# Splitting the first query and key loads over three queues, and moving one relu ahead of a cast, in a fused attention and gated-FFN kernel

## The chip, the cores and the metric

The kernel runs on one core of a Trainium2 chip. The metric is the device time in microseconds (us) of one execution. Before the change the median of three runs was 435.25 us (434.73 to 435.25). A profile shows one execution; its engines are TensorE (PE, with its weight loads as PEld), VectorE (DVE), ScalarE (ACT), GpSimd (POOL) and SyncE (SP). SP, ACT and POOL each have a queue of their own for DMAs.

## The reference

```
scores = (q @ k^T) / sqrt(64)              # 8 batches, 12 heads, 448 rows, 64 columns
attn   = max(scores, 0)^2 / 448            # no softmax
x      = (attn @ v), heads side by side    # 3584 rows x 768
gate   = max(x @ w_gate, 0)                # 768 -> 1536
val    = x @ w_val
out    = (gate * val) @ w_out              # 1536 -> 768
```

All inputs and the output are float32. The kernel computes in bf16 with float32 accumulation, and applies both constant factors once, squared together, when the output leaves PSUM (L294).

## The kernel before

The eight batches are handled one after the other. A batch's attention is made of score tiles of 128 keys by two heads (2 x 448 queries, one tile of two PSUM banks, tag sc, three buffers), a relu on ACT from PSUM to SBUF (L184, tile r_sb, four buffers), a square on DVE (L188, tile attn), and products with v. Heads go in pairs hp (0 to 5), and two pairs make a group qd of four heads. The FFN of a batch is a list of units: twelve gv_unit (gate and value products for 128 of the 1536 columns, L257) and then out_unit (output products, L283). From batch 1 on these units are dealt out between the attention steps, so that TensorE has matmuls while ACT and DVE work on the scores. Batch 0 has no FFN beside it: first_batch (L378) runs alone, and eight gv_units follow it.

Every instruction is pinned: each engine runs its instructions in the order in which the program lists them. Waits between engines follow from the data and the buffers.

Keys and queries arrive with rows across partitions (tiles kn and qn, [128, head, 4, 64]: partitions 0 to 63 hold four consecutive rows each, rows 0 to 255; partitions 64 to 127 hold three each, rows 256 to 447). So each load is a pair of DMAs, lo and hi. Loads on POOL's queue (dma_in, L95) cast float32 to bf16 on the way. For batches 0 to 2 TensorE transposes two heads of k and q at a time into a PSUM bank (L177), and DVE copies 960 columns (512 for k, 448 for q, the last 64 of k's 512 being padding) to SBUF (L179, tile kq_sb). Later batches are transposed by DMA, by way of the buffers kr and qr.

The start is special. load_first(4) (L97) brings the keys of heads 0 to 3 as float32 into staged, a view of the then unused buffer kr, by SP's queue (lo, L101) and ACT's (hi, L102); DVE casts them two heads at a time into kn (L107). The queries of those heads come by POOL. Then POOL makes the identity for the transposes (L91) and issues k and q of heads 4 to 7, k and q of heads 8 to 11, v, and the weights in chunks (L333 to L344). ACT, right behind its DMA, runs one relu on a blank tile (L104), which makes it load its function table early. TensorE runs 14 pairs of matmuls on blanks (L395) before the first transposes and some more between the first rounds.

In first_batch, five rounds (n = 0 to 4) make three score tiles each, transpose the next head pair, and relu and square the tiles. After that comes a tail written out by hand (L409 to L430). It has score tiles u0 to u2 (of n = 5) and w0 to w2 (of n = 6), and six products values(qd, c) with v, each in a PSUM bank of tag acc (two buffers), turned into the FFN's input xT by a cast: four on DVE, and those of values(1, 0) and values(2, 0) on ACT:

```
relu2(*u1)
w0 = tile_of(6, 0)
cast(*values(1, 0), on_act=True)
relu2(*u2)
w1 = tile_of(6, 1)
```

relu2 is one relu on ACT and one square on DVE. With the banks' reuse, the first gate product (g_ps) needs the bank of values(2, 0).

Of the kernel before, what the change touches and what calls it, by code (L numbers as in the profile page):

```python
# [9 lines left out]
FP32 = mybir.dt.float32  # L10
BF16 = mybir.dt.bfloat16
# [5 lines left out]
def kernel(  # L17
# [15 lines left out]
    nc = tc.nc  # L33

    B, H, S, D = q.shape
# [16 lines left out]
    kqpool = ctx.enter_context(tc.tile_pool(name="kqpool", bufs=3))  # L52
# [7 lines left out]
    def pin(ins):  # L60
        return tc.keep_in_program_order(ins)
# [15 lines left out]
    kn_b = [const.tile([128, H, 4, D], BF16, name=f"kn{i}") for i in range(NB)]  # L77
    qn_b = [const.tile([128, H, 4, D], BF16, name=f"qn{i}") for i in range(NB)]
    v_b = [const.tile([128, H, 4, D], BF16, name=f"vn{i}") for i in range(NB)]
    kr = const.tile([128, 4, d_model], BF16, name="kr")  # L80
    qr = const.tile([128, 4, d_model], BF16, name="qr")
    staged = kr.rearrange("p i m -> p (i m)")[:, 0:4 * 8 * D].bitcast(FP32)
    staged = staged.rearrange("p (h i d) -> p h i d", i=4, d=D)
    for n in range(NB):
        if n == 0:
            pin(nc.vector.memset(staged[64:128, :, 3, :], 0.0))
        for t in (kn_b[n], qn_b[n]):
            pin(nc.vector.memset(t[64:128, :, 3, :], 0.0))

    def make_ident():  # L90
        pin(nc.gpsimd.affine_select(out=ident, in_=ident, compare_op=ALU.not_equal, fill=1.0, base=0,  # L91
                                    pattern=[[-1, 128]], channel_multiplier=1))

    def dma_in(o, i):
        pin(nc.gpsimd.dma_start(out=o, in_=i))  # L95

    def load_first(h1):  # L97

        lo = k[0, 0:h1, 0:256, :].rearrange("h (j i) d -> j h i d", i=4)
        hi = k[0, 0:h1, 256:448, :].rearrange("h (j i) d -> j h i d", i=3)  # L100
        pin(nc.sync.dma_start(out=staged[0:64], in_=lo))  # L101
        pin(nc.scalar.dma_start(out=staged[64:128, :, 0:3, :], in_=hi))  # L102

        pin(nc.scalar.activation(rpool.tile([128, 2, S], BF16, name="r_sb")[:, 0, :], blank, AF.Relu))  # L104
        load_nat(qn_b[0], q, 0, 0, h1)
        for h in range(0, h1, 2):
            pin(nc.vector.tensor_copy(kn_b[0][:, h:h + 2], staged[:, h:h + 2]))  # L107

    def load_nat(dst, src, b, h0, h1):
        lo = src[b, h0:h1, 0:256, :].rearrange("h (j i) d -> j h i d", i=4)  # L110
        hi = src[b, h0:h1, 256:448, :].rearrange("h (j i) d -> j h i d", i=3)
        dma_in(dst[0:64, h0:h1, :, :], lo)
        dma_in(dst[64:128, h0:h1, 0:3, :], hi)

    def load_qk(b, h0=0, h1=H):
        load_nat(kn_b[b % NB], k, b, h0, h1)
        load_nat(qn_b[b % NB], q, b, h0, h1)

    def load_v(b):
        load_nat(v_b[b % NB], v, b, 0, H)  # L120

    def low_values(b):

        t = v_b[b % NB].rearrange("p (q s h) i d -> p q s h i d", s=2, h=2)
        pin(nc.vector.tensor_copy(t[64:128, :, 1, :, 3, :], t[0:64, :, 1, :, 3, :]))
# [31 lines left out]
    def operands(b, hp, bank=None):  # L157

        if b >= PE_B:
            n = b % NB  # L160
            return kT_b[n][:, hp, 0:S], qT_b[n][:, hp, 0:S]
        kq = transposes(b, hp, bank)
        return kq[:, 0:S], kq[:, 512:512 + S]

    def sc_tile():
        return psum.tile([128, 2, 512], FP32, name="sc_ps", tag="sc", bufs=3)
# [1 line left out]
    def transposes(b, hp, bank):  # L168
        if bank is None:
            ps = psum.tile([128, 2048], BF16, name="kq_ps", tag="sc", bufs=3)  # L170
        else:
            ps = bank.bitcast(BF16)
        for t, c0 in ((kn_b[b % NB], 0), (qn_b[b % NB], 512)):
            for i in range(4):
                for h2 in range(2):
                    o = ps[h2 * 64:h2 * 64 + 64, c0 + i * 128:c0 + i * 128 + 128]
                    pin(nc.tensor.transpose(o, t[:, 2 * hp + h2, i, :], ident))  # L177
        kq = kqpool.tile([128, 512 + S], BF16, name="kq_sb")
        pin(nc.vector.tensor_copy(kq, ps[:, 0:512 + S]))  # L179
        return kq  # L180

    def relu_part(src, n):
        r = rpool.tile([128, 2, S], BF16, name="r_sb")[:, :n, :]
        pin(nc.scalar.activation(r, src, AF.Relu))  # L184
        return r

    def square_part(dst, r):
        pin(nc.vector.tensor_tensor(dst, r, r, ALU.mult))  # L188

    def relu2(src, dst, n):  # L190
        square_part(dst, relu_part(src, n))
# [31 lines left out]
    def av_pair(b, qd, c, attn, ps):  # L223

        p = HALVES[c][1]
        for h2, o in HALVES:
            mm(ps[o, :S], v_b[b % NB][p, 4 * qd + 2 * c + h2, 3, :], attn[p, 6 + h2, :], True, False)
        for i in range(3):
            for h2, o in HALVES:
                mm(ps[o, :S], v_b[b % NB][:, 4 * qd + 2 * c + h2, i, :], attn[:, 8 * c + 2 * i + h2, :], False, i == 2)  # L230

    def bank_tile():
        return psum.tile([128, 512], FP32, name="xT_ps", tag="acc", bufs=2)

    def idle_matmuls(ps, n):

        for _ in range(n):
            mm2(ps[:, :S], blank[:, 0:128], blank, True, True)
# [86 lines left out]
    def gap():  # L325
# [4 lines left out]
        flush()  # L330
        share[2] = i + 1

    load_first(4)  # L333
    make_ident()
    load_qk(0, 4, 8)
    load_qk(0, 8, H)
    load_v(0)
    load_gv(0)
    load_gv(1)
# [14 lines left out]
    def transpose_pair(b, hp, bank=None):  # L354
        kqs[b, hp] = operands(b, hp, bank)

    def attn_of(b, qd):
        if (b, qd) not in attns:
            attns[b, qd] = atpool.tile([128, 14, S], BF16, name="attn")
        return attns[b, qd]  # L360

    def burst(b, tiles):

        todo, begun = [], None
        for qd, kind, c, i in tiles:
            attn = attn_of(b, qd)
            if kind == "pair":
                todo.append(scores(kqs[b, 2 * qd + c], i, attn, 8 * c + 2 * i))
            elif kind == "last":
                todo.append(scores_last((kqs[b, 2 * qd], kqs[b, 2 * qd + 1]), attn))  # L370
            else:
                ps = sc_tile()
                banks = [ps[:, c, :S] for c in range(2)]
                av_last(b, qd, attn, banks)
                begun = (qd, banks, ps[:, :, :S])
        return todo, begun

    def first_batch():  # L378

        def tile_of(n, i):  # L380
            return burst(0, [tiles_first[3 * n + i]])[0][0]

        def values(qd, c):
            ps, x = bank_tile(), xT_of[0][:, 2 * qd + c, :]
            av_pair(0, qd, c, attn_of(0, qd), ps)
            return x, ps[:, :S]

        def cast(x, ps, on_act=False):
            if on_act:
                pin(nc.scalar.activation(x, ps, AF.Copy))  # L390
            else:
                pin(nc.vector.tensor_copy(x, ps))

        bank = bank_tile()
        idle_matmuls(bank, 14)  # L395
        transpose_pair(0, 0, bank)
        bank = bank_tile()
        idle_matmuls(bank, 4)
        for n in range(5):
            t = [tile_of(n, i) for i in range(3)]  # L400
            if n == 4:
                low_values(0)
            transpose_pair(0, n + 1, bank)
            if n < 4:
                bank = bank_tile()
                idle_matmuls(bank, 2)
                for u in t:
                    relu2(*u)
        relu2(*t[0])  # L409
        relu2(*t[1])  # L410
        u0 = tile_of(5, 0)
        cast(*values(0, 0))
        relu2(*t[2])
        u1 = tile_of(5, 1)
        cast(*values(0, 1))
        u2 = tile_of(5, 2)
        relu2(*u0)
        relu2(*u1)
        w0 = tile_of(6, 0)
        cast(*values(1, 0), on_act=True)  # L420
        relu2(*u2)
        w1 = tile_of(6, 1)
        cast(*values(1, 1))
        w2 = tile_of(6, 2)
        relu2(*w0)
        relu2(*w1)
        x, ps = values(2, 0)
        relu2(*w2)
        cast(x, ps, on_act=True)
        cast(*values(2, 1))  # L430
# [45 lines left out]
    for b in range(B):  # L476
        xT_of[b] = xpool.tile([128, KD, S], BF16, name="xT")
        if b == 0:
            first_batch()
        else:  # L480
            batch(b)
        if b + 1 < B:
            ffn.extend(ffn_units(b))
            if b == 0:
                for _ in range(7):
                    ffn.pop(0)()
                for hp in range(2):
                    midway.append(lambda hp=hp: transpose_pair(1, hp))
                ffn.pop(0)()
# [34 lines left out]
```

## Time and profile before

| | us |
|---|---|
| median of three runs | 435.25 |
| the profiled execution, in whole | 435.1 |
| its span in the profile | 433.3 |
| PE busy | 425.4 (98%) |
| PEld busy | 250.3 (58%) |
| ACT busy | 218.0 (50%) |
| DVE busy | 210.7 (49%) |
| POOL busy | 49.0 (11%) |
| first score relu starts | 7.74 |
| first gate product starts | 27.04 |

The granted TensorE clock is 0.9 or more of full speed in all forty slices of the span. The DMA engines are busy 90% or more in each of the first eight slices, which is up to about 87 us, and have gaps after that. A row of the timeline gives the start, the length (of the whole group when several are merged), engine, line, operation, output and input, and in brackets the idle time ahead of it with what ended it. A share of DMA above 1 means several packets in flight on an engine. The size of a DMA, and GB/s, count bytes as written: a load that casts float32 to bf16 reads twice as many (47.19 MB were read from memory in all). A busy PE is not a PE at its peak, since the ends of pipelined matmuls are modelled; the waits say more than the shares.

### The profile page before, as it was taken

What the parts mean: (1) busy time and instruction counts of PE and PEld (TensorE: products, weight loads), DVE (VectorE), ACT (ScalarE), POOL (GpSimd) and SP (SyncE); (2) the same over time, 40 slices, a digit from 0 to 9 for tenths busy, and PEclk for the clock granted to TensorE, in tenths of its full rate; (3) what the DMA queues carried; (4) which work ended last, traced back from release to release, by engine and by line L of the source; (5) the groups of instructions that cost most, each with busy time, mean ns of one, the idle gap of its engine ahead of it and who ended that gap; (6) DMA issues with size and microseconds to landing.
All of it is one profiled execution on the core that took longest, in us unless ns stands there. A gap on an engine that the chain in (4) does not pass through costs nothing.

```text
span 433.3 us, 11436 instructions
## 1 busy us (share of the span) xinstructions
PE 425.4 (98%) x5068; PEld 250.3 (58%) x5068; DVE 210.7 (49%) x334; ACT 218.0 (50%) x325; POOL 49.0 (11%) x71
## 2 busy tenths in 40 slices
PE   8899999999999999999999999999999999999996
PEld 4457655655565555655566555655566555566564
DVE  5952784556623655356532565435643454422210
ACT  4942666454554564465454645554545645532221
POOL 8424311100204000300004000010000000000001
PEclk9999999999999999999999999999999999999999
DMA  9999999905679770591517932170414100030014
GB/s 151 181 205 195 203 205 211 204 5 81 106 145 166 103 112 19 104 198 34 97 38 128 176 66 65 38 138 2 101 29 106 42 2 2 12 100 2 2 38 109
DMA packets 78513, 42.45 MB, mean 98 GB/s; under 512 B 48352, under 2 KB 74976, under 8 KB 78464
## 3 DMA queue, kind: packets, MB, share of 16 engines
q0 software_dynamic: 45120, 23.47, 40.6%
q1 hardware_dynamic: 32992, 18.01, 17.8%
q8 instruction: 39, 0.64, 0.6%
q10 hardware_dynamic: 352, 0.25, 0.2%
q14 instruction: 10, 0.08, 0.1%
HBM read 47.19 MB, written 11.01 MB: 134 GB/s over the span
## 4 chain that ended last, share of the span: by engine, by line
PE 84%; DMA 12%; POOL 2%; issue 1%; POOLq 0%; ACT 0%
PE o_ps L64 25%; PE g_ps L64 23%; PE v_ps L64 22%; PE sc_ps L64 13%; DMA qn<-in_q_dram 5%; DMA wo<-in_moe_w_out_dram 5%; DMA vn<-in_v_dram 2%; POOL qn L95 1%; PE kq_ps L177 1%; POOL kn L95 1%; POOL vn L95 0%; POOL out_dram L302 0%; POOLq L519 0%; ACT o_sb L294 0%; POOL ident L91 0%
## 5 line engine op out<-in xcount | busy, mean ns | idle before, releaser
L184 ACT ACTIVATE r_sb<-sc_ps 128x896 bf16<-128x896 f32 x168 | 145.1, 927 | 39.4 <-PE sc_ps L64 39.4
L188 DVE TENSOR_TENSOR attn<-r_sb 128x896 bf16<-128x896 bf16 x168 | 103.7, 623 | 92.2 <-ACT r_sb L184 92.1
L64 PE MATMUL g_ps<-xT,wg 128*64 128x448 bf16 x1152 | 126.1, 354 | 0.0
L64 PE MATMUL v_ps<-xT,wv 128*64 128x448 bf16 x1152 | 125.2, 352 | 0.0
L64 PE MATMUL o_ps<-wo,hT 128*64 128x384 bf16 (+1 forms) x1368 | 115.3, 324 | 0.3 <-DMA wo<-in_moe_w_out_dram 0.3
L271 DVE TENSOR_TENSOR hT<-v_ps,g_sb 128x448 bf16<-128x448 f32 x96 | 59.9, 624 | 88.4 <-PE v_ps L64 87.5
L64 PEld LDWEIGHTS <-hT 128*64 128x64 bf16 x1368 | 75.5, 110 | 37.8 <-issue 6.5
L265 ACT ACTIVATE g_sb<-g_ps 128x448 bf16<-128x448 f32 x96 | 52.3, 545 | 88.9 <-PE g_ps L64 88.9
L64 PEld LDWEIGHTS <-wg 128*64 128x64 bf16 x1152 | 63.4, 110 | 49.8 <-issue 13.1
L64 PEld LDWEIGHTS <-wv 128*64 128x64 bf16 x1152 | 66.2, 110 | 41.0
L294 ACT ACTIVATE o_sb<-o_ps 128x384 f32<-128x384 f32 (+1 forms) x57 | 27.9, 489 | 81.4 <-PE o_ps L64 81.4
L64 PE MATMUL sc_ps<-attn,vn 128*64 128x448 bf16 (+1 forms) x336 | 35.1, 354 | 0.0
L95 POOL DMA_DIRECT2D vn<-in_v_dram x16 | 12.1, 768 | 168.5 <-PE sc_ps L64 161.0
L458 DVE CAST xT<-sc_ps 128x896 bf16<-128x896 f32 x21 | 22.9, 1091 | 14.3 <-PE sc_ps L64 14.3
L64 PEld LDWEIGHTS <-vn 128*64 128x64 bf16 (+1 forms) x384 | 18.8, 109 | 16.5 <-issue 5.6
L64 PE MATMUL sc_ps<-qT,kT 64*64 64x448 bf16 x420 | 28.4, 357 | 0.0
L64 PE MATMUL sc_ps<-kq_sb 64*64 64x448 bf16 x252 | 19.0, 360 | 1.9 <-ACT r_sb L184 1.7
L95 POOL DMA_DIRECT2D kn<-in_k_dram x18 | 13.3, 762 | 46.8 <-PE kq_ps L177 45.2
L64 PEld LDWEIGHTS <-kT 64*64 64x64 bf16 x420 | 9.6, 105 | 14.3 <-issue 11.7
L302 POOL DMA_DIRECT2D out_dram<-o_sb x2 | 1.1, 558 | 146.2 <-ACT o_sb L294 146.2
L95 POOL DMA_DIRECT2D qn<-in_q_dram x20 | 14.6, 752 | 9.4 <-DMA vn<-in_v_dram 6.3
L64 PEld LDWEIGHTS <-kq_sb 64*64 64x64 bf16 x252 | 6.5, 105 | 13.3 <-issue 9.9
(32 smaller groups left out, 84.2 us busy)
## 6 DMA issues: line engine op xcount, KB each, us to landing
out_dram<-o_sb SPq DMA_DIRECT2D x54, 192.0 KB, 2.7
vn<-in_v_dram POOLq DMA_DIRECT2D x8, 384.0 KB, 7.7
kn<-in_k_dram POOLq DMA_DIRECT2D x7, 384.0 KB, 9.7
qn<-in_q_dram POOLq DMA_DIRECT2D x7, 384.0 KB, 12.2
vn<-in_v_dram POOLq DMA_DIRECT2D x8, 288.0 KB, 8.7
wo<-in_moe_w_out_dram POOLq DMA_DIRECT2D x2, 1152.0 KB, 20.0
kn<-in_k_dram POOLq DMA_DIRECT2D x7, 288.0 KB, 10.9
qn<-in_q_dram POOLq DMA_DIRECT2D x7, 288.0 KB, 13.0
```

The source lines that it names most:

```text
L64: pin(nc.tensor.matmul(o, lhsT=l, rhs=r, start=start, stop=stop, skip_group_check=True))
L95: pin(nc.gpsimd.dma_start(out=o, in_=i))
L177: pin(nc.tensor.transpose(o, t[:, 2 * hp + h2, i, :], ident))
L184: pin(nc.scalar.activation(r, src, AF.Relu))
L188: pin(nc.vector.tensor_tensor(dst, r, r, ALU.mult))
L265: pin(nc.scalar.activation(g_sb, g_ps, AF.Relu))
L271: pin(nc.vector.tensor_tensor(hT[:, mf, col:col + S], v_ps, g_sb, ALU.mult))
L294: pin(nc.scalar.activation(out=o_sb[:, c0:c1], in_=o_ps, func=AF.Copy, scale=float(out_scale)))
L302: pin(e.dma_start(out=segment_rows(b0, 2 * t + s)[:, m], in_=o_sb[s * 64:s * 64 + 64, m]))
L458: pin(nc.vector.tensor_copy(xT_of[b][:, 2 * qd:2 * qd + 2, :], both))
```

## The change

Four things are changed.

- load_first now has three pairs of float32 loads on SP's and ACT's queues: keys of heads 0 and 1, queries of heads 0 and 1, keys of heads 2 and 3. A second view, of the buffer qr, stages the queries, and two of its heads get a clearing memset. POOL brings only the queries of heads 2 and 3 there. DVE has three casts instead of two.
- POOL then loads the keys of heads 4 to 11 in one pair of DMAs, followed by the queries of heads 4 to 7 and of heads 8 to 11. Before, it was two pairs for keys and two for queries.
- In the tail of the first batch ACT's relu of tile u2 comes ahead of ACT's cast of values(1, 0). TensorE's and DVE's order stays.
- kq_sb holds 2 x 448 columns instead of 960, and the copy reads two pieces of 448 out of PSUM.

```diff
--- before.py
+++ after.py
@@ -79,11 +79,14 @@
     v_b = [const.tile([128, H, 4, D], BF16, name=f"vn{i}") for i in range(NB)]
     kr = const.tile([128, 4, d_model], BF16, name="kr")
     qr = const.tile([128, 4, d_model], BF16, name="qr")
-    staged = kr.rearrange("p i m -> p (i m)")[:, 0:4 * 8 * D].bitcast(FP32)
-    staged = staged.rearrange("p (h i d) -> p h i d", i=4, d=D)
+    staged = []
+    for grp in (kr, qr):
+        st = grp.rearrange("p i m -> p (i m)")[:, 0:4 * 8 * D].bitcast(FP32)
+        staged.append(st.rearrange("p (h i d) -> p h i d", i=4, d=D))
     for n in range(NB):
         if n == 0:
-            pin(nc.vector.memset(staged[64:128, :, 3, :], 0.0))
+            pin(nc.vector.memset(staged[0][64:128, :, 3, :], 0.0))
+            pin(nc.vector.memset(staged[1][64:128, 0:2, 3, :], 0.0))
         for t in (kn_b[n], qn_b[n]):
             pin(nc.vector.memset(t[64:128, :, 3, :], 0.0))
 
@@ -94,17 +97,19 @@
     def dma_in(o, i):
         pin(nc.gpsimd.dma_start(out=o, in_=i))
 
-    def load_first(h1):
-
-        lo = k[0, 0:h1, 0:256, :].rearrange("h (j i) d -> j h i d", i=4)
-        hi = k[0, 0:h1, 256:448, :].rearrange("h (j i) d -> j h i d", i=3)
-        pin(nc.sync.dma_start(out=staged[0:64], in_=lo))
-        pin(nc.scalar.dma_start(out=staged[64:128, :, 0:3, :], in_=hi))
+    def load_first():
+
+
+        for st, src, h in ((staged[0], k, 0), (staged[1], q, 0), (staged[0], k, 2)):
+            lo = src[0, h:h + 2, 0:256, :].rearrange("h (j i) d -> j h i d", i=4)
+            hi = src[0, h:h + 2, 256:448, :].rearrange("h (j i) d -> j h i d", i=3)
+            pin(nc.sync.dma_start(out=st[0:64, h:h + 2], in_=lo))
+            pin(nc.scalar.dma_start(out=st[64:128, h:h + 2, 0:3, :], in_=hi))
 
         pin(nc.scalar.activation(rpool.tile([128, 2, S], BF16, name="r_sb")[:, 0, :], blank, AF.Relu))
-        load_nat(qn_b[0], q, 0, 0, h1)
-        for h in range(0, h1, 2):
-            pin(nc.vector.tensor_copy(kn_b[0][:, h:h + 2], staged[:, h:h + 2]))
+        load_nat(qn_b[0], q, 0, 2, 4)
+        for st, t, h in ((staged[0], kn_b[0], 0), (staged[1], qn_b[0], 0), (staged[0], kn_b[0], 2)):
+            pin(nc.vector.tensor_copy(t[:, h:h + 2], st[:, h:h + 2]))
 
     def load_nat(dst, src, b, h0, h1):
         lo = src[b, h0:h1, 0:256, :].rearrange("h (j i) d -> j h i d", i=4)
@@ -160,7 +165,7 @@
             n = b % NB
             return kT_b[n][:, hp, 0:S], qT_b[n][:, hp, 0:S]
         kq = transposes(b, hp, bank)
-        return kq[:, 0:S], kq[:, 512:512 + S]
+        return kq[:, 0, :], kq[:, 1, :]
 
     def sc_tile():
         return psum.tile([128, 2, 512], FP32, name="sc_ps", tag="sc", bufs=3)
@@ -175,8 +180,8 @@
                 for h2 in range(2):
                     o = ps[h2 * 64:h2 * 64 + 64, c0 + i * 128:c0 + i * 128 + 128]
                     pin(nc.tensor.transpose(o, t[:, 2 * hp + h2, i, :], ident))
-        kq = kqpool.tile([128, 512 + S], BF16, name="kq_sb")
-        pin(nc.vector.tensor_copy(kq, ps[:, 0:512 + S]))
+        kq = kqpool.tile([128, 2, S], BF16, name="kq_sb")
+        pin(nc.vector.tensor_copy(kq, ps[:, 0:1024].rearrange("p (t c) -> p t c", t=2)[:, :, 0:S]))
         return kq
 
     def relu_part(src, n):
@@ -330,10 +335,11 @@
         flush()
         share[2] = i + 1
 
-    load_first(4)
+    load_first()
     make_ident()
-    load_qk(0, 4, 8)
-    load_qk(0, 8, H)
+    load_nat(kn_b[0], k, 0, 4, H)
+    load_nat(qn_b[0], q, 0, 4, 8)
+    load_nat(qn_b[0], q, 0, 8, H)
     load_v(0)
     load_gv(0)
     load_gv(1)
@@ -417,8 +423,9 @@
         relu2(*u0)
         relu2(*u1)
         w0 = tile_of(6, 0)
-        cast(*values(1, 0), on_act=True)
+        second = values(1, 0)
         relu2(*u2)
+        cast(*second, on_act=True)
         w1 = tile_of(6, 1)
         cast(*values(1, 1))
         w2 = tile_of(6, 2)
```

## The prediction

> **What bounds the kernel now.** I read the chain that ended last first, then who TensorE waits for, then the chain again in order of time, then the instructions of the first 30 us, and last the DMA rate by stretch.
>
> The chain's shares by engine:
> ```profile
> PE 84%; DMA 12%; POOL 2%; issue 1%; POOLq 0%; ACT 0%
> ```
> All TensorE's waits in the whole run (total, times, longest):
> ```profile
> PE sc_ps L64 <- ACT r_sb L184: 1.7, 5, 0.4
> PE xT_ps L64 <- DVE blank L74: 1.2, 1, 1.2
> PE xT_ps L64 <- DVE attn L188: 0.7, 2, 0.4
> PE o_ps L64 <- DMA wo<-in_moe_w_out_dram: 0.3, 1, 0.3
> ```
> The chain in order of time, its first 65 us:
> ```profile
> 6.70 1.23 POOL qn L95 x2
> 7.92 0.63 POOL vn L95
> 8.55 10.05 DMA vn<-in_v_dram
> 18.60 0.28 issue
> 18.88 22.11 DMA qn<-in_q_dram
> 41.00 0.86 issue
> 41.85 21.70 DMA wo<-in_moe_w_out_dram
> 63.55 0.04 issue
> 63.60 1.17 PE o_ps L64 x12
> ```
> The reader should see three stretches. Up to 27 us TensorE waits for others. From 27.04 us to the end it is never kept waiting, but for once: the second half of w_out lands at 63.55, and the first output product, ready at 63.34, starts at 63.60 (0.26 us). So the chain that ended last does not run through the first batch at all: it runs through the loads. Whatever the first batch gains, call it G, brings that product's readiness forward to 63.34 - G, but it can't start before w_out is there. If the loads come D earlier, the gain at the end is the smaller of D and G + 0.26.
>
> The first batch, rows of the timeline:
> ```profile
> 5.33 1.01 DVE L107 CAST kn<-kr 128x512 bf16<-128x512 f32 x2 [2.14 <-DMA kr<-in_k_dram]
> 6.59 0.66 DVE L179 COPY kq_sb<-xT_ps 128x960 bf16<-128x960 bf16 x1 [0.26 <-PE xT_ps L177]
> 7.74 13.88 ACT L184 ACTIVATE r_sb<-sc_ps 128x896 bf16<-128x896 f32 x17 [4.36 <-PE sc_ps L64]
> 22.36 0.54 ACT L390 ACTIVATE xT<-xT_ps 128x448 bf16<-128x448 f32 x1 [0.74 <-PE xT_ps L64]
> 26.17 0.62 DVE L188 TENSOR_TENSOR attn<-r_sb 128x896 bf16<-128x896 bf16 x1 [0.18 <-ACT r_sb L184]
> 27.04 1.33 PE L64 MATMUL g_ps<-xT,wg 128*64 128x448 bf16 x12
> ```
> ACT is the bound of this stage: it runs 17 relus without a gap from 7.74 to 21.62, then stands 0.74 us for the value product that its cast needs.
>
> The loads, one stretch a row (length; busy us of PE, PEld, DVE, ACT, POOL; clock; DMA share; GB/s written):
> ```profile
> 8.00:9.00 1.00, 1.00 (x25) 0.64 (x21) 0.32 (x1) 1.00 (x2) 1.00 (x2) 1.00 1.45 176
> 12.00:14.00 2.00, 1.63 (x28) 0.83 (x28) 1.83 (x4) 2.00 (x3) 2.00 (x3) 1.00 1.26 148
> 20.00:25.00 5.00, 4.46 (x50) 1.69 (x46) 4.54 (x9) 4.26 (x6) 0.83 (x1) 1.00 1.24 207
> 30.00:40.00 10.00, 10.00 (x110) 7.40 (x107) 2.73 (x5) 2.42 (x5) 3.21 (x5) 1.00 1.48 196
> ```
> From about 2.5 us on the DMA engines have work all the time; only the rate differs, 362 GB/s at best while the first keys come as float32, 176 for the queries and keys after them, 139 on average from 10.5 to 14.5, then about 200.
>
> **The change part by part.** The profiled execution took 435.1 us, its span 433.3 and 1.8 around it; the median of the three runs is 435.25, their spread 0.52. The sum is made against 435.1.
>
> *Relu ahead of ACT's cast.* ACT is free at 21.62 and the scores of u2 were made at 20.87 to 21.25, so relu u2 fills the gap (pitch of relus 0.80 us) and the cast follows at about 22.42, beside the product ready at 22.31. Three relus after it by 0.80 end at 25.4 instead of 26.14. Late next would be DVE: its square of u2 moves from 23.74 to 23.22, right behind the square of u1 (ends 23.28); the cast of values (1,1) and the squares of w0 and w1 follow at a pitch of 0.54, so the square of w2 starts at 25.42 instead of 26.17. TensorE's wait for relu u2 at 23.76 (0.26 us) goes too. What is queued behind the moved relu is the cast that frees a bank, needed only by values (2,0), now at 23.9. Gain at the first gate product: 0.74 us.
>
> *First loads.* Before, k of heads 0 to 3 landed at 5.24 on SP's queue (issue 0.74, 4.5 to landing) and at 4.0 on ACT's; POOL's q of heads 0 to 3 at 6.05. Now three pairs go out on each of the two queues. One more issue costs its queue about 0.75 us (0.77 and 0.74 in the timeline). SP issues nothing else until 69 us. On ACT two more issues push the table load and the blank relu from 1.51 to about 3.0, done near 4.9; ACT's next work is at 7.74, so 2.8 us of cover hide 1.5 us. The extra clearing of two heads on DVE is half of a 0.27 us row, hidden before the first cast at 5.33. The queries' cast is new on DVE, one at about 0.5 us (two cost 1.01). TensorE can't start the transposes before the 28 idle matmuls let it, at 5.45 (0.19 behind the last, as between all of them), against 5.81: at most 0.36 to win. But DVE's queue now holds three casts ahead of the first copy, and the third, keys of heads 2 and 3, waits for the last pair. The HW queues carried 0.459 MB, the last bytes at about 4.3, landing 5.24; 0.229 MB more at 200 to 362 GB/s take 0.63 to 1.15 us, less some 0.4 since the first pair is half as long and SP's bytes, which began only at 3.0 behind ACT's, come sooner. So it lands between 5.5 and 6.0, its cast ends between 6.05 and 6.55, against a copy that started at 6.59 and at best starts at 6.23. Gain 0 to 0.36; a landing past 6.1 makes it a loss, to -0.2. I take 0.1, nearer to the contended rate, as POOL's queue begins to move at 3.7.
>
> *896-column copies.* 0.66 us for 960 columns scales to 0.62 for 896: 0.03 on the first copy, and nothing on the 17 others, hidden behind ACT (three relus take 2.43 us a round, DVE's copy and squares 2.26) or behind matmuls. The copy's two pieces of 448 could be slower than one piece. Against that stands L151, 3072 bf16 elements in runs of 64 in 0.95 us. From above: at the pace of the 448-column float32 casts (0.62 each) a copy would take about 1.1. I take 0.62.
>
> So G is 0.74 + 0.1 + 0.03, about 0.85 (0.5 to 1.15).
>
> *POOL's issues.* A four-head pair has a pitch of 1.20 us (3.00, 4.20, 5.40, 6.60, 7.80), the twelve-head pair of v 1.48. By a line through these an eight-head pair is 1.34 and a two-head pair 1.13. Two four-head pairs become one of eight (-1.06) and the first shrinks (-0.07): v and all the weights are issued 1.1 us earlier. Later issues each wait until the eighth load before them has landed (the 19th load, q of batch 1, starts at 17.16 behind v's first half, the 11th), and two loads fewer shift both alike.
>
> *What D is.* This is the disputed cost. As an issue matter D is up to 1.1. But POOL handed out 0.229 MB each 1.20 us, 191 GB/s, while 177 were moved, and time to landing grew from 3.7 to 4.4 us over those issues: the engines are slightly behind POOL, so most of the 1.1 isn't theirs to give. As a matter of bytes: queries of two heads leave POOL's queue (0.115 MB written at 177 GB/s, 0.65 us) and come as float32 (0.229 MB at 362 GB/s, 0.63 us): nothing. Counted as bytes written at the later 196 to 207 GB/s, the extra 0.115 MB costs 0.57 us. A gain lies in the pace: 177 GB/s at a share of 1.43 in 4 to 10 us against 196 at 1.48 when much was queued ahead (30 to 40 us). If larger and earlier issues bring the remaining 1.03 MB of keys and queries to 195, that is 5.83 - 5.29 = 0.54 us. Ends: -0.57 and +1.1. I take +0.3, about half of the pace's gain: the latency shows backlog, so near the middle. Sum: 435.1 - min(0.3, 1.1) = 434.8.
>
> The Trainium skill, page "DMA: Bandwidth & Descriptors", section "Issuing engines are not separate DMA queues", says that loads of all issuing engines run on the same 16 engines and interleave, and that spreading them saves only issue time. The rows agree in that 362 GB/s read is about twice the 177 written after a halving cast; by that page alone D is 0 and the time is the second rival's.
>
> **The rivals.**
> 1. The loads were paced by POOL: D reaches the cap G + 0.26 = 1.1, time 434.0 (433.7 with G 1.15). For it: the pace of 177 is near 191, and the slow stretch of 10.5 to 14.5 us ends when POOL stops issuing at 14.24, which now comes 1.1 us sooner. Against: the growing latency.
> 2. The transfer is hidden anyway: D = 0, the product waits 0.26 + G instead of 0.26, time 435.1. For it: equal bytes read, engines with work from 2.5 us on. Against: pace below that of 30 to 40 us.
> 3. Slower: w_out lands later, since the float32 queries add written bytes ahead of everything. D = -0.57, time 435.7; any D below 0 decides, because TensorE has no slack at 63.6. To come out past 0.2% it needs -0.9, so a further stall of the kind seen at 10.5 to 14.5 (139 against 196 GB/s is 1.2 us of 4): 436.3 with half of it added. Against: the float32 rows move at twice the written rate.
> 4. The cut copy falls to 1.1 us: five rounds of 2.7 instead of 2.43 and 0.45 on the first, 1.8 us lost, G = -0.95, time 435.8.
>
> **How the numbers follow.** A measurement of this kernel can tell about 0.2%, 0.87 us, from no change; faster then means below 434.4. Forecast (434.4 to 435.0) 0.38; rival 1 0.32; rival 2 0.14; rival 3 0.12; rival 4 0.04. Faster: rival 1 and a little of the forecast's edge, 0.34. Slower by over 0.2%: the part of rival 3 with a further stall and of rival 4, 0.10. Same: the rest, 0.56. The range from 433.8 to 435.9 leaves out the best case of rival 1 and the worst of rival 3. The likeliest one's own is 434.4 to 435.0.
>
> **What would show it.** Right: ACT's 0.74 gap at the cast gone, 18 relus in one run; the first gate product near 26.2; POOL's first weight issue near 8.2; and TensorE's wait for w_out at 63 us grown from 0.26 to about 0.8. Wrong: w_out landing before 62.6 (rival 1), after 63.7 (rival 3), rows of L179 above 0.7 us (rival 4), or the first copy later than 6.6 behind the third cast. Wrong as a whole if TensorE has no wait for w_out left, or new waits after 64 us.

## The result and the profile after

The changed kernel took 435.87 us (median of 20 runs, 435.14 to 436.99), the kernel before 434.91 (median of 20, 434.59 to 435.38). The ratio is 1.0019, with an interval of 1.0012 to 1.0026: the change makes the kernel slower by 0.96 us. The forecast was 0.3 us faster. The profiled execution of the changed kernel took 436.1 us, its span 434.3.

TensorE's waits after, the whole run (total, times, longest):

```profile
PE sc_ps L64 <- ACT r_sb L189: 1.6, 4, 0.4
PE xT_ps L64 <- DVE blank L74: 1.2, 1, 1.2
PE xT_ps L182 <- DVE qn L112: 1.0, 1, 1.0
PE sc_ps L64 <- DVE kq_sb L184: 0.3, 1, 0.3
PE xT_ps L64 <- DVE attn L193: 0.2, 1, 0.2
```

The wait for w_out is gone. In its place TensorE waits for DVE's cast of the queries (L112), and for the first copy (L184). The chain that ended last, in order of time, now begins at SP's queue:

```profile
1.57 0.82 SPq L106
2.39 0.04 issue
2.43 5.82 DMA kr<-in_k_dram
8.26 0.03 issue
8.28 0.02 DVEq L112
8.30 0.04 issue
8.35 0.43 DVE kn L112
8.78 0.54 DVE kq_sb L184
9.32 0.04 issue
9.36 0.76 PE sc_ps L64 x12
```

The reader should see the third pair of float32 loads, keys of heads 2 and 3, issued at 2.43 and landing only at 8.26. Its cast stands on DVE ahead of the first copy, which was done at 7.25 before and is done at 9.31 now, for heads 0 and 1, which don't need those keys. But that cast is the smaller part of the delay. The queries of heads 0 and 1, which the first copy does need, landed at 7.27, and TensorE's transposes of them ended at 8.27, against 6.55 before. Of the 2.10 us by which the first copy starts later (8.69 against 6.59), the late queries make 1.7 and the third cast 0.4. The timeline's rows of the first batch:

```profile
4.29 0.43 DVE L112 CAST kn<-kr 128x512 bf16<-128x512 f32 x1 [0.96 <-DMA kr<-in_k_dram]
7.36 0.45 DVE L112 CAST qn<-qr 128x512 bf16<-128x512 f32 x1 [2.64 <-DMA qr<-in_q_dram]
8.35 0.43 DVE L112 CAST kn<-kr 128x512 bf16<-128x512 f32 x1 [0.54 <-DMA kr<-in_k_dram]
8.69 0.62 DVE L184 COPY kq_sb<-xT_ps 128x896 bf16<-128x896 bf16 x1
9.65 0.83 POOL L98 DMA_DIRECT2D wg<-in_moe_w_gate_dram  x1 [1.20 <-DMA kn<-in_k_dram]
9.80 14.69 ACT L189 ACTIVATE r_sb<-sc_ps 128x896 bf16<-128x896 f32 x18 [5.09 <-PE sc_ps L64]
24.41 0.54 ACT L396 ACTIVATE xT<-xT_ps 128x448 bf16<-128x448 f32 x1
28.28 1.33 PE L64 MATMUL g_ps<-xT,wg 128*64 128x448 bf16 x12
```

ACT's gap ahead of its cast is gone, and 18 relus run without a break. But the first relu starts at 9.80 instead of 7.74, and the first gate product at 28.28 instead of 27.04. Two differences make up the first gate product's delay of 1.24 us: 2.06 lost before the first relu, and 0.82 won between it and the gate product (18.48 us after, 19.30 before). The two spans differ by 1.0 and not by 1.24, since the 0.26 us that TensorE waited for w_out in the profile of before are gone.

Sizes and microseconds to landing of the early loads after, for issues at 1.57 to 2.4 us:

```profile
qr<-in_q_dram SPq DMA_DIRECT2D x1, 128.0 KB, 5.7
qr<-in_q_dram ACTq DMA_DIRECT2D x1, 96.0 KB, 3.4
kr<-in_k_dram ACTq DMA_DIRECT2D x1, 96.0 KB, 5.7
qn<-in_q_dram POOLq DMA_DIRECT2D x1, 64.0 KB, 3.1
qn<-in_q_dram POOLq DMA_DIRECT2D x1, 48.0 KB, 5.4
```

and for SP's third, issued at 2.43:

```profile
kr<-in_k_dram SPq DMA_DIRECT2D x1, 128.0 KB, 5.8
```

Before, SP's single load of 256 KB had landed after 4.5 us:

```profile
kr<-in_k_dram SPq DMA_DIRECT2D x1, 256.0 KB, 4.5
```

Now half of that size takes 5.7 or 5.8, from issue to landing.

### The profile page after: what moved, and what is told of

Same layout as the page of the kernel before. It is cut to its first block, busy times and chain, and to the rows that moved or that the text cites. A ratio compares the mean times of both kernels' runs of the same rounds, so it can differ in the third digit from the quotient of the medians.

```text
span 434.3 us, 11444 instructions
## 1 busy us (share of the span) xinstructions
PE 426.2 (98%) x5068; PEld 250.2 (58%) x5068; DVE 210.3 (48%) x336; ACT 218.0 (50%) x325; POOL 48.0 (11%) x69
## 4 chain that ended last, share of the span: by engine, by line
PE 93%; DVE 3%; DMA 1%; issue 1%; ACT 1%; SPq 0%; POOL 0%; POOLq 0%; DVEq 0%
PE g_ps L64 26%; PE o_ps L64 25%; PE v_ps L64 25%; PE sc_ps L64 15%; DVE attn L193 2%; DMA kr<-in_k_dram 1%; PE kq_ps L182 1%; ACT r_sb L189 1%; DVE kq_sb L184 1%; DVE xT L398 0%; SPq L106 0%; PE xT_ps L182 0%; DVE hT L276 0%; POOL out_dram L307 0%; POOLq L526 0%
## 5 line engine op out<-in xcount | busy, mean ns | idle before, releaser
L98 POOL DMA_DIRECT2D kn<-in_k_dram x16 | 12.0, 764 | 48.7 <-PE kq_ps L182 47.5
L98 POOL DMA_DIRECT2D qn<-in_q_dram x20 | 14.5, 748 | 4.8 <-DMA vn<-in_v_dram 2.3
```

## The experiments

The theory after the result: the float32 loads land late because POOL's loads share the DMA engines with them; the relu's move is worth what was forecast; w_out is no cap. The first rival: the second and third load of a queue are slow by themselves. The second: the wait for w_out limits the kernel, and the parts act through it. "First relu" and "first gate" below are starts in the profiled execution of each kernel.

### The parts taken alone or together, loads as before

The edit of the first, against the kernel before:

```diff
-        return kq[:, 0:S], kq[:, 512:512 + S]
+        return kq[:, 0, :], kq[:, 1, :]
...
-        kq = kqpool.tile([128, 512 + S], BF16, name="kq_sb")
-        pin(nc.vector.tensor_copy(kq, ps[:, 0:512 + S]))
+        kq = kqpool.tile([128, 2, S], BF16, name="kq_sb")
+        pin(nc.vector.tensor_copy(kq, ps[:, 0:1024].rearrange("p (t c) -> p t c", t=2)[:, :, 0:S]))
...
-        cast(*values(1, 0), on_act=True)
+        second = values(1, 0)
         relu2(*u2)
+        cast(*second, on_act=True)
```

> The moved relu and the 896-column copies alone, with all loads as before. Theory (the start is late in the changed kernel because of the float32 loads; w_out is early there because of POOL's loads): first score relu at 7.7, first gate product near 26.25 (0.77 sooner), w_out lands near 63.5 as before, TensorE's wait for it grows from 0.26 to about 1.0, time within 0.2 us of before. Rival (the loads run ahead because the first batch does): w_out lands before 63.0 and the time falls by 0.5 us or more.

434.11 us against 434.89 before, ratio 0.9985 (0.9976 to 0.9994). First relu to first gate took 18.49 us. In this execution the first relu was itself late, at 8.53, which the last section comes back to, so the gate product started at 27.02 and not at 26.25. w_out landed at 63.3. That execution took 434.83 us, 0.72 above the kernel's median, so its rows are not those of a typical one. By the medians of 11 and 21 runs the time fell by 0.78 us: a forecast of no gain, on the grounds that w_out holds everything back, was wrong a second time.

Next, the relu's three lines of this edit alone, and the copies' lines alone, each against the kernel before:

> The moved relu alone. Theory (all of the 0.78 us that relu and copies gave together is the relu's): ACT's gap of 0.74 before its cast gone, first relu to first gate product 18.5 us instead of 19.3, time 0.7 to 0.8 below before. Rival (the shorter copies share in it): 0.4 us or less.

> The 896-column copies alone. Theory: 0.62 us a copy instead of 0.66, first relu to first gate product 19.3 us as before, time within 0.2 us of before. Rival (they share in the gain): 0.3 us or more below before.

The relu alone took 434.23 against 434.77, ratio 0.9985 (0.9976 to 0.9994), 18.49 us from first relu to first gate. The copies alone took 434.79, ratio 0.9999 (0.9990 to 1.0008), 19.30 us. By the medians the relu gave 0.54 us, less than the 0.7 to 0.8 expected and more than its rival's 0.4; the interval, about 0.3 to 1.0 us, holds the 0.78 as well. The copies alone show no gain, though the noise would hide one of 0.4. So the gain is the relu's as far as these runs can tell, and the timeline gives its size. It is 0.81 and not 0.74 on the timeline because a gap counts from an end to a start, while neighbours on ACT overlap: after, the cast starts at 24.41 and the relu ahead of it ends at 24.49.

### The new loads alone

The changed kernel with both parts above undone.

> The new loads alone, without the moved relu and with the 960-column copies. Theory: first score relu near 9.8 as in the changed kernel, first gate product near 29.05 (28.28 plus 0.77), no wait for w_out, time 0.8 us above the changed kernel, that is about 1.7 above before. Rival (the relu's move is worth less, since something else ends the first batch): less than 0.4 us above the changed kernel.

436.77 us against 434.89, ratio 1.0039 (1.0027 to 1.0052). First relu 9.68, first gate 28.98, 19.30 us between them. TensorE's waits:

```profile
PE xT_ps L182 <- DVE qn L112: 2.2, 1, 2.2
PE sc_ps L64 <- ACT r_sb L189: 1.7, 5, 0.4
```

So the loads cost 1.88 us by themselves, and the relu and the copies give 0.78 back; that makes 1.1 for the whole, against 0.96 measured. The time lies 0.90 above the changed kernel, near the 0.8 of the theory. This profile is also a repeat of the changed kernel's start: the queries of heads 0 and 1 landed at 7.2 and the keys of heads 2 and 3 at 7.9. With the first loads as before, the first relu starts between 7.74 and 8.53 in six profiles, so the loss before it is 1.2 to 2.1 us.

### What makes the float32 loads late

First POOL's loads were held back. The changed kernel, with the identity made first and one small copy on POOL that needs the last float32 load:

```diff
+        hold = const.tile([128, 2, 64], FP32, name="hold")
+        pin(nc.gpsimd.tensor_copy(hold, staged[0][:, 2:4, 0, :]))
         load_nat(qn_b[0], q, 0, 2, 4)
...
+    make_ident()
     load_first()
-    make_ident()
```

> The changed kernel, but POOL makes the identity and then reads the staged keys of heads 2 and 3 before it issues its first load, so that SP's and ACT's loads are alone on the DMA engines. Theory 1 (they are late because POOL's loads share the DMA engines): the queries of heads 0 and 1 land by 5.2 instead of 7.3, the keys of heads 2 and 3 by 5.9 instead of 8.2. Theory 2 (the second and third load of a queue are slow by themselves): they land at 7.3 and 8.2 again. In both the time is some 3 to 4 us above before, as all other loads start some 5 us later.

The same loads, issued at 1.50 to 2.43 us, in this kernel:

```profile
qr<-in_q_dram SPq DMA_DIRECT2D x1, 128.0 KB, 3.8
kr<-in_k_dram SPq DMA_DIRECT2D x1, 128.0 KB, 3.4
qr<-in_q_dram ACTq DMA_DIRECT2D x1, 96.0 KB, 3.4
kr<-in_k_dram ACTq DMA_DIRECT2D x1, 96.0 KB, 3.4
```

Alone on the engines, the queries landed at 5.4 and the keys of heads 2 and 3 at 5.8, and the first relu started at 7.53, earlier than before the change. So nothing in the queues themselves makes the second and third load late. The whole took 439.57 us (one run), 4.7 above before where 3 to 4 had been expected, since all of POOL's loads came 5 us later and the later rounds waited for them.

Then only POOL's big key pair and what follows it were held, and the queries of heads 2 and 3 went out at once:

```diff
     make_ident()
+    hold = const.tile([128, 2, 64], FP32, name="hold")
+    pin(nc.gpsimd.tensor_copy(hold, staged[0][:, 2:4, 0, :]))
     load_nat(kn_b[0], k, 0, 4, H)
```

> The changed kernel, POOL issuing the queries of heads 2 and 3 at once as there, but reading the staged keys of heads 2 and 3 before it issues any further load. Theory (the trailing bytes of SP's and ACT's loads are held up by POOL's big key pair, which flows from 5 us): queries of heads 0 and 1 land by 5.6 and keys of heads 2 and 3 by 6.3. Rival (the 0.1 MB of queries from POOL is enough to do it): they land after 6.5 and 7.

```profile
qr<-in_q_dram SPq DMA_DIRECT2D x1, 128.0 KB, 4.1
kr<-in_k_dram SPq DMA_DIRECT2D x1, 128.0 KB, 3.9
```

The queries landed at 5.7 and the keys at 6.3, as the theory said. That brought the first relu to 7.89 and the whole to 437.04 us (one run), as the later rounds waited for POOL's held loads. And the key pair was taken apart again, as before the change:

```diff
-    load_nat(kn_b[0], k, 0, 4, H)
-    load_nat(qn_b[0], q, 0, 4, 8)
-    load_nat(qn_b[0], q, 0, 8, H)
+    load_qk(0, 4, 8)
+    load_qk(0, 8, H)
```

> The changed kernel with one part undone: the keys and queries of heads 4 to 11 in four-head pairs as before. Theory (the single key pair is not what delays the start): queries of heads 0 and 1 land near 7.3, first relu near 9.7, time as the changed kernel within 0.3 us. Rival (the eight-head pair crowds the float32 loads): they land by 6.3, first relu by 8.5, time about 434.8.

```profile
qr<-in_q_dram SPq DMA_DIRECT2D x1, 128.0 KB, 4.4
kr<-in_k_dram SPq DMA_DIRECT2D x1, 128.0 KB, 5.1
```

This one took 435.51 us, ratio to before 1.0008 (0.9999 to 1.0017), first relu at 9.19. The four kernels make a series, one profile each (landing times are issue plus time to landing, the later of the two queues):

| POOL's loads in flight beside the float32 ones | queries of heads 0, 1 land | keys of heads 2, 3 land |
|---|---|---|
| none | 5.4 | 5.8 |
| queries of heads 2 and 3 | 5.7 | 6.3 |
| these, then four-head pairs | 6.0 | 7.5 |
| these, then one eight-head pair (the change) | 7.3 | 8.2 |

The more POOL has in flight, the later the float32 loads land, and the eight-head pair is the worst. My expectation for the last experiment, that undoing it would change nothing, missed at the loads: the queries landed 1.3 us sooner, as its rival said. The first relu came only 0.6 sooner, between the two, because the keys' cast still stood ahead of the first copy and held it for 1.0 us. In time it gave 0.36 us back by the medians, and the two ratios to before (1.0008 and 1.0019) have intervals that overlap, so this part is not clear of noise. The larger part of the loss is there with four-head pairs too: 435.51 (1.0008 of before) against 434.11 (0.9985) for the relu and copies with the first loads as before.

How the queues share the engines is in the traces. From 3 to 4 us in the changed kernel POOL's queue moved 145 packets, SP's 121 and ACT's 114, about equal shares. From 6 to 7 us:

```profile
q0 software_dynamic: 216, 0.10, 82.4%
q1 hardware_dynamic: 28, 0.03, 9.6%
q10 hardware_dynamic: 28, 0.02, 8.4%
```

(packets, MB, share of 16 engines; q0 is POOL's queue, q1 SP's, q10 ACT's.) The last bytes of the float32 loads came through at a trickle while POOL's queue moved most of the packets.

By the Trainium skill, page "DMA: Bandwidth & Descriptors", section "Queues, rings and completion order", each DMA engine takes turns between the queues that have work for it, packet by packet. The packets of 3 to 4 us agree with that, as does the series: a load on SP's queue isn't served ahead of POOL's that were issued after it. The unequal counts of 6 to 7 us would need the engines one by one, which no run here shows.

### One key pair, with the first loads as before

The relu, the copies and the eight-head pair; the queries of heads 0 to 3 by POOL.

> The moved relu, the copies and the one pair of loads for the keys of heads 4 to 11; the first loads as before, with the queries of heads 0 to 3 by POOL. Theory A (the single pair brought w_out forward by 1 us): w_out lands near 62.6, first gate product near 26.25, time about 434.0, 0.9 below before. Theory B (the float32 queries on the other queues brought it forward): w_out lands near 63.5, time as before.

434.06 us, ratio 0.9981 (0.9972 to 0.9990). w_out landed at 60.96, 2.6 us sooner than in the first profile of before. Yet the time is that of the relu and copies without it (434.11). The time came out as theory A said, but not for its reason: w_out's landing carried none of it. This kernel is the fastest median of those tried, 0.83 us below before, and not told apart from the relu and copies alone.

### The float32 loads split, for keys only

In the kernel of the last experiment, the keys of heads 0 to 3 go as two pairs on SP's and ACT's queues, and the queries of heads 0 to 3 as two pairs by POOL:

```diff
+        for h in range(0, h1, 2):
+            lo = k[0, h:h + 2, 0:256, :].rearrange("h (j i) d -> j h i d", i=4)
+            hi = k[0, h:h + 2, 256:448, :].rearrange("h (j i) d -> j h i d", i=3)
+            pin(nc.sync.dma_start(out=staged[0:64, h:h + 2], in_=lo))
+            pin(nc.scalar.dma_start(out=staged[64:128, h:h + 2, 0:3, :], in_=hi))
...
-        load_nat(qn_b[0], q, 0, 0, h1)
+        for h in range(0, h1, 2):
+            load_nat(qn_b[0], q, 0, h, h + 2)
```

> Moved relu, copies and one key pair, and the float32 loads are again the keys of heads 0 to 3 alone, but as two pairs of two heads on SP's and ACT's queues; POOL brings the queries of heads 0 and 1 and of heads 2 and 3 as two pairs. Theory (what delays the start is the float32 queries' extra bytes on the shared DMA engines): keys of heads 2 and 3 land by 6.0, first relu by 7.7, time 433.8 to 434.1. Rival (any later load on these queues is delayed once POOL's loads flow): keys of heads 2 and 3 land after 7, the first copy waits behind their cast, first relu after 8.5, time 434.8 or more.

434.29 us against 435.05, ratio 0.9986 (0.9977 to 0.9995), a little above the 433.8 to 434.1 expected. The keys of heads 2 and 3 landed near 5.4 and the first relu started at 7.50, as the theory said: without the queries' float32 bytes two pairs on these queues are on time. The experiment does not part two causes, though: POOL also issued its eight-head pair 1.2 us later here, at 4.10 instead of 2.93. Of the early start 0.27 us were given back. POOL's queries of heads 4 and 5 came late, which TensorE's waits show:

```profile
PE xT_ps L179 <- DMA qn<-in_q_dram: 0.7, 1, 0.7
```

so that ACT stood once more and the first gate came at 26.26, 18.76 us after the first relu.

### The kernel before, once more

> The kernel before, once more, to see how far its own profile moves. If the wait for w_out in its first profile belongs to the kernel, w_out lands near 63.5 again and TensorE waits about 0.3 for it; if it belongs to that one execution, w_out lands sooner and there is no such wait, as with the relu and copies alone.

TensorE's waits in this second profile of the unchanged kernel:

```profile
PE sc_ps L64 <- ACT r_sb L184: 1.7, 5, 0.4
PE xT_ps L64 <- DVE blank L74: 1.2, 1, 1.2
PE xT_ps L64 <- DVE attn L188: 0.7, 2, 0.4
```

and its rows of the load of w_out's second half and of the output products:

```profile
39.96 0.83 POOL L95 DMA_DIRECT2D wo<-in_moe_w_out_dram  x1 [1.41 <-DMA qn<-in_q_dram]
62.12 1.17 PE L64 MATMUL o_ps<-wo,hT 128*64 128x384 bf16 x12
63.56 1.14 PE L64 MATMUL o_ps<-wo,hT 128*64 128x384 bf16 x12
```

There is no wait for w_out. It was issued 1.9 us sooner than in the first profile, at 39.96 against 41.85, and landed at 62.3 against 63.55 (22.3 to landing), in the same kernel. This execution took 435.03 us, the first 435.1. With the early loads as they were, w_out landed at 63.55, 62.3, 63.3, 62.6 and 62.65 in five profiles (before twice, relu and copies, relu alone, copies alone). A wait for it shows as a larger distance between the first two output products: 1.88 in the first profile and 1.67 with the relu and copies, 1.44 or 1.45 in the other three. Among the other seven profiles only the keys-only split has it, with 1.74 and w_out at 62.6. So such a wait comes and goes.

## Why the prediction was wrong, step by step

**The forecast was put on the wrong term.** The prediction's rule was that the end moves by the smaller of D and G + 0.26. That rule is not what failed. In the changed kernel's profile D was 1.03 (w_out at 62.52 against 63.55) and G was -1.24 (first gate product at 28.28 against 27.04), and the rule gives a loss of 0.98; the two profiled executions differ by 1.0, the medians by 0.96. What failed is the sizes. D was taken as 0.3 and as the smaller term, from a wait in one execution that was held to be the kernel's own. The second profile of before doesn't have it, and w_out's landing moves by 1.3 us between two executions of one program, more than any D that was considered. A late w_out does hold the product in three of the twelve profiles, but it costs little: from the first gate product to the end of the span it is 406.08 to 406.26 us in these three and 405.75 to 406.08 in the other nine. So what the time follows, to within 0.5 us, is G.

**The first loads were mis-sized, and this alone turned the sign.** The step that failed is "0.229 MB more at 200 to 362 GB/s take 0.63 to 1.15 us, less some 0.4", hence a landing "between 5.5 and 6.0" and a loss of at most 0.2. The keys of heads 2 and 3 landed 3.0 us later than before the change, at 8.26, and the first relu started 2.06 us later. For the second pair, the queries of heads 0 and 1, the prediction gave no landing at all; they came at 7.27, and they account for 1.7 us of the first copy's delay. So G, taken as +0.85, came out as -1.24. The figures of 5.5 and 6.0 are what the loads do alone (5.8 for the keys). The traffic beside them was noticed, "as POOL's queue begins to move at 3.7", but it was priced as a lower rate for the added bytes. What the series shows is that the tail of every load that is not yet done is held up, while POOL keeps adding. DVE's order added 0.4 us, and that part was foreseen: the third cast ahead of the first copy, and "the first copy later than 6.6 behind the third cast" stood among the signs of a wrong prediction. No run moves that cast behind the first copy, so the 0.4 is read from the rows. The late landing needed a rival of its own, at 8; the list had none.

**POOL's issues.** v was issued at 6.72 instead of 7.80, the 1.1 us foretold. The weights were not: the first one, POOL's 11th load, waited 1.20 us for the key pair, whose first half is the 3rd, to land and went out at 9.65, later than the 9.28 of before. The prediction's rule of the eighth load before was applied to the later loads only. In the kernel with one key pair and the first loads as before there was no such wait, and that weight went out at 8.24.

**The relu** was right: 0.74 forecast, 0.81 in the profiles of five kernels, and a time that fits it (0.54 to 0.78 by the medians). **The copies** were right: 0.62 us each and, within the noise of 0.4, nothing at the end.

**The rivals.** The first (loads paced by POOL) saw w_out's landing move by the size it named, to no effect, and that move lies within the 1.3 us between two executions of before. The third had the right sign, but its way was late w_out, and w_out came sooner. The fourth is excluded by the 0.62 us. The measured 435.87 lies just inside the upper end of 435.9, and got there by a way that had been given no more than 0.2 us; that the range holds it is luck.

## What to carry to other kernels

A wait of 0.3 us in one profile is not a property of the kernel: before a forecast is hung on it, ask how far the thing waited for moves between executions, above all where it is the end of a long queue of transfers. When the end is the smaller of two gains, size the worst case of both. A load put on a second queue is not served first; count what the other queues have in flight until it lands, give every transfer that the first work needs a landing of its own, and put nothing that waits for the last one ahead of that work. When the price of contention has no row, the floor is a rival of its own, not a small discount.

## What the hardware showed unexpectedly

The first 28 matmuls on blanks took 4.53 us in the first profile of before and 5.44 in that of the changed kernel. They ended up to 1.1 us apart over all twelve profiles (4.31 to 5.44), in no order that follows the edits. Weight loads of before at 4.5 us and of the changed kernel at 6.0:

```profile
4.52 0.74 PEld L64 LDWEIGHTS <-blank 128*64 128x64 bf16 x8 [0.19 <-issue]
```

```profile
6.01 0.18 PEld L182 LDWEIGHTS <-kn 128*64 128x64 bf16 x2 [0.20 <-issue]
```

Eight in a row without a gap, in 0.74 us, at 4.52 in the one; still two at a time, each two with a gap as long as they are, 0.38 us together, at 6.01 in the other. That is half the pace. TensorE came to full pace more than 1.5 us later, while the granted clock in the rows reads 1.00 throughout. With the relu and copies, where the loads landed as before (the keys 4.5 us after their issue), this moved the first relu from 7.74 to 8.53. In the changed kernel it was hidden, since the queries came later still. The Trainium skill, page "TensorE: Matmul & The Clock Gate", section "Part 1: The HAM clock gate (the "warmup" mystery)", says that the array starts at half pace and that the moment of release varies from run to run, since the window that decides it runs freely. The profiles agree with the half pace and with the variation; the window itself no run here shows.

A second one stays open. The DMA rate has a slow stretch whose place moves. In the first profile of before it was at 10.5 to 14.5 us (139 GB/s); the second profile, with the same loads, has no such stretch there:

```profile
12.00:14.00 2.00, 1.59 (x32) 0.87 (x32) 1.99 (x4) 2.00 (x4) 2.00 (x3) 1.00 1.48 185
```

(length; busy us of PE, PEld, DVE, ACT, POOL; clock; DMA share; GB/s). The changed kernel has one at 5 to 7 us:

```profile
5.00:6.00 1.00, 1.00 (x8) 0.43 (x6) 0.00 (x0) 0.00 (x0) 1.00 (x2) 1.00 1.03 152
6.00:7.00 1.00, 0.88 (x12) 0.51 (x8) 0.00 (x0) 0.00 (x0) 1.00 (x3) 1.00 1.00 149
```

and after it the rate was 196 where the first profile of before had 148. The new loads alone have it there too (131 and 155 GB/s). With four-head pairs the same two microseconds read:

```profile
5.00:6.00 1.00, 1.00 (x8) 0.45 (x6) 0.00 (x0) 0.00 (x0) 1.00 (x3) 1.00 1.01 214
6.00:7.00 1.00, 1.00 (x22) 0.80 (x20) 0.43 (x1) 0.00 (x0) 1.00 (x3) 1.00 1.37 188
```

The keys-only split, which has the eight-head pair and two float32 pairs, shows it most (94 and 84), while the one key pair with the first loads as before does not (162 and 161, against 169 and 177 in the first profile of before). So at 5 to 7 us the slow stretch is in all three kernels that have both the split loads and the eight-head pair, with nothing held back, and in two of them it falls just where the float32 loads' last bytes were waited for. The last step of the series above, from 6.0 to 7.3 us, may be this stretch as much as the bytes in flight; no run parts them. POOL issues in the slow stretches and in the fast ones too, so its issuing alone doesn't make one. What does was not found: the traces tell the queues apart but not the sixteen engines.
